# The first token group of a state-space block with a PReLU layer, put in another order

## The chip, the cores and the metric

The kernel runs on one core of a Trainium2 chip. The metric is the device time of one execution in microseconds. Five engines with a queue of their own each work in parallel: PE (matrix products), DVE (vector), ACT (scalar, activations), POOL (GpSimd) and SP (which issues most transfers). Each works through its own instructions strictly in order and waits for the others by semaphores.

## The reference

```
for each batch, head and chunk of 32 steps (4 batches, 8 heads, 768 steps):
    L     = exp(cum_i - cum_j), lower triangle, cum = running sum of log(clip(a, 1e-6, 1))
    y     = (C B^T * L) x  +  (C state) * exp(cum)
    state = exp(sum) * state + sum_j B_j x_j exp(cum_end - cum_j)
x2  = y as a (3072 tokens x 256) matrix, heads side by side
h   = x2 @ w_in                                  # 256 x 2048
g   = max(h, 0) + alpha * min(h, 0)              # PReLU, alpha per column
out = g @ w_out                                  # 2048 x 256
```

The weights w_in and w_out arrive as 64-bit floating-point numbers, the other arrays as 32-bit ones. The result is 32-bit.

## The kernel before

**Tiling.** The kernel works with its own chunks of 128 steps, 24 of them, two to a pair. Two pairs make a group of 512 tokens, and there are six groups. The state-space part of a pair gives its 256 columns of the matrix xT (features x tokens). When a group's xT is whole, the PReLU layer runs on it. Groups 1 to 5 use a product with fewer multiplications (`quad`, in four stretches for each group, with sums and differences of weights and tokens). Group 0 is different, because the weights are still arriving: it runs plain products, one tile of 128 hidden columns after another. All the changes concern group 0 and the loading that goes on beside it.

**Weights.** The weights come in 16 pieces of 512 KB. Pieces 0, 1 and then 2, 4, 6, 8, 10, 12 are parts of w_in (two tiles of hidden columns each), and 3, 5, 7, 9, 11, 13, 14, 15 are parts of w_out (two tiles each). Six buffers (`raw`) hold pieces as they land. A piece is turned into 32-bit numbers by several engines in turn: `convert_a` (ACT L238, then POOL L240, and ACT L245 or two L248), `sign` (DVE L259), `convert_b` (DVE L269) and the final addition in `convert` (POOL L291). The function `convert_next` finishes the next piece and, when its buffer is free again, issues the load of the piece six further on. Called with `first` it also begins `convert_a` two pieces ahead.

**First two pairs.** `first_two` computes pairs 0 and 1 by hand-written order, and with them the first two hidden tiles in halves (`hidden_two`: matmul L870, ACT L876, DVE L882). Its helpers are `turned` (transposes of B and C, copied by ACT into bc and cz), `gram_of` (L679), `added` (L688), `mask` (POOL L695), `copied` (ACT L703), `times` (L708 on POOL or DVE), `decays` (DVE scan L712) and `outputs` (L727, L735, and the copies to xT at L740; `warm` puts idle products ahead of them).

**The loop over tiles.** After that a loop runs over tiles f = 4 to 15. In each round come `hidden(0, f)` (matmul L855, ACT L858, DVE L859), some stages of the next pair (`ssm`: transposes L550, state L513 and L526, decay scans L470, gram L599, L609, outputs L628 and L636), the conversion of weight pieces, and `output` of the tile four earlier (L893). Two buffers (`hp`) take the hidden products, so tile f + 2 waits until DVE has read tile f, and a pair's gram borrows one of the two. Pair 2 and pair 3 are computed in this loop, for group 1.

**Later rows.** The decay factors of batches 2 and 3 come from a tile `rows` by clamping and two scans (`rows_clamp`, `rows_scan`, `rows_out`: L372 to L393). Their results go to memory, and pairs from 6 on read them from there. In the kernel before this happens in round 8 of the loop.

**Order.** There is no scheduler: every engine's instructions stand in the order in which the code issues them. SP issues nearly all loads in one queue. Names with one buffer number can be reused only when their readers are done.

Of the kernel before, what the change touches and what calls it, by code (L numbers as in the profile page):

```python
# [9 lines left out]
F32 = mybir.dt.float32  # L10
# [12 lines left out]
def kernel(  # L23
# [25 lines left out]
    nc = tc.nc  # L49
# [69 lines left out]

    def load_rows(i):  # L120

        rows = ld.tile([RW, Q], F32, name="rows")
        nc.sync.dma_start(out=rows, in_=a.rearrange("b h (c t) -> (b h c) t", t=Q)[i * RW : (i + 1) * RW])
        loads["r", i] = rows
# [15 lines left out]
    def load_pair(gp, decays=True):  # L140
# [8 lines left out]
        if gp == 0:  # L149
            load_a(ap, b, c, nc.scalar)  # L150
        elif gp >= NB:
            rows = scratch["pf", b // 2].rearrange("(b h c) t -> b h (c t)", b=2, h=H)
            rows = rows[b % 2, :, c * Q : (c + 2) * Q]
            nc.sync.dma_start(out=ap, in_=rows.unsqueeze(1).to_broadcast([H, N, 2 * Q]))
        if gp == 0:
            load_rows(0)
            nc.sync.dma_start(out=al_n, in_=moe_alpha.rearrange("(k p) -> k p", p=P))
# [326 lines left out]
    def pair(gp):  # L484
# [9 lines left out]
        def decays(k):  # L494

            for w in range(2):
                half_decays(k, w)
# [84 lines left out]
        else:  # L582
            states(added(ss_tile()))
            c_decayed()
            decays(0)
            yield
            decays(1)
            spread_c()

# [59 lines left out]
    def first_two():  # L649
# [43 lines left out]
        def mask(sm, new, ks):  # L693
            n = ks.stop - ks.start
            nc.gpsimd.tensor_tensor(  # L695
                out=sm[:, ks].rearrange("p k (g m) -> p k g m", g=2),
                in0=new[:, ks].unsqueeze(2).to_broadcast([P, n, 2, 2 * D]),
                in1=hmask.rearrange("p (g m) -> p g m", g=2).unsqueeze(1)
                .to_broadcast([P, n, 2, 2 * D]), op=ALU.mult)
# [64 lines left out]
        for r in range(4):  # L764
# [15 lines left out]
               for i in range(2)]  # L780
# [4 lines left out]
        nc.scalar.copy(out=new[0][:, 0], in_=dps[0][:, 0])  # L785
        sm0 = work.tile([P, 2, P], F32, name="sm")
        times(0, 0, g0, nc.gpsimd)
        mask(sm0, new[0], slice(0, 1))
        g1 = copied(gram[1])
        times(0, 1, g1, nc.gpsimd)  # L790
        convert_a(*pieces[0])
        times(0, 2, gram[2])
# [7 lines left out]
        convert_a(*pieces[1])  # L800
        outputs(0, (ss(), ss()), (None, sm0[:, 0]), cd0, xt0, (1, 0), 2)
        mask(sm0, new[0], slice(1, 2))
        bn1 = bn_of(1)

        sign(*pieces[0])
# [3 lines left out]
        convert_next()  # L809
        slope_signs()  # L810
        sign(*pieces[1])
        decays(1, 0, sp[1][0])
        convert_b(*pieces[1])
        tp = spare()
        bc1, cz1 = turned(nat1, tp)
        cd1 = work.tile([P, 2, Q], F32, name="cd")
        nc.gpsimd.tensor_tensor(out=cd1.rearrange("p k t -> p (k t)"),
                                in0=bc1[:, 2:].rearrange("p k t -> p (k t)"), in1=pf1,
                                op=ALU.mult)
        added(dps[1], bn1, xt1)  # L820
        new[1] = work.tile([P, 2, 2 * D], F32, name="state")
        for k in range(2):
# [3 lines left out]
                                           in1=dps[1][:, k], op0=ALU.mult, op1=ALU.add)  # L826
        decays(1, 1, sp[1][1])
        prelus = [hidden_two(0, 0, 0, tp)]
        gram = gram_of(bc1, cz1, [bank(2), bank(3), ss(), ss()])
        g0 = copied(gram[0])  # L830
        convert_next(first=False)
        sm1 = work.tile([P, 2, P], F32, name="sm")
        mask(sm1, new[1], slice(0, 2))
        times(1, 0, g0, nc.gpsimd)
        for r in range(1, 4):
            times(1, r, gram[r])
# [4 lines left out]
        prelus[1]()  # L841
        outputs(1, (bank(0), bank(1)), (sm0[:, 1], sm1[:, 0]), cd1, xt1, (0, 1), 1)
        state[0] = new[1][:, 1]
# [314 lines left out]
    first_two()  # L1158
    convert_a(*pieces[3])
    convert_next(first=False)  # L1160
    hidden_two(0, 0, 2 * Q, spare())()
    rest = hidden_two(0, 2, 2 * Q, spare())
# [3 lines left out]
    bns[2] = pair_loads(2)  # L1166
    convert_next(first=False)
    in_steps = {8: 0, 10: 1, 12: 2, 14: 3}
    for f in range(FIRST, NF):
        if f in (5, 10):  # L1170
            load_pair(3 + f // 10)
        if f == 5:
            load_rows(1)
        hidden(0, f)
        if f <= 10:
            ssm(2)
        if f >= 9:
            ssm(3)
        for i in {FIRST: (5,), FIRST + 1: (6, 7)}.get(f, ()):
            convert_a(*pieces[i])  # L1180
        convert_next(first=f > FIRST)
        if f == 14:
            bns[4] = pair_loads(4)
        if f == 8:
            bns[3] = pair_loads(3)
        if f == 8:
            rows_clamp(1)
            held["pr"] = rows_scan(1)
            rows_out(1)
        output(f - FIRST)  # L1190
        if f in in_steps:
            weight_sums(wi, in_sums, 0, in_steps[f])
    early[0] = None
    token_sums(1)
    ssm(2 * GC // 2, 4)
# [93 lines left out]
```

## Time and profile before

| What | us |
|---|---|
| median of 10 runs | 363.36 |
| lowest and highest of 10 runs | 362.53 to 364.48 |
| the profiled execution | 363.79 |
| its span, from the first to the last instruction | 362.1 |
| first hidden matmul (L870) | 18.10 |
| first matmul of the loop (L855, tile 4) | 29.12 |
| first matmul of group 1 (L979) | 82.69 |

The profile is of one execution. A row of a timeline gives the start, the duration (of all instructions merged in it), the engine, the line of the program, the operation, the output and the inputs, shapes, and in square brackets how long the engine was idle before it and what ended that. A row of waits gives the waiting engine, tile and line, what it waited for, the total, the number of waits and the longest. A row of the table by stretches gives the limits of the stretch and their length, the busy time of PE, of PE's weight loads, of DVE, ACT and POOL with the number of instructions of each, the granted clock of PE, the share in which the DMA engines were busy, and GB/s.

### The profile page before, as it was taken

Reading aid. Unit: us, or ns where it says so; the run is one execution under the profiler, and the core shown is the slowest. Engines: PE = TensorE matmul, PEld = TensorE weight load, DVE = VectorE, ACT = ScalarE, POOL = GpSimd, SP = SyncE. Lnnn points to the kernel's source line nnn. Section 1 sums busy time; section 2 is a strip of 40 time slices with the busy share of each in tenths; the row PEclk is TensorE's granted clock in tenths of the full one; section 3 lists DMA queues with packets and bytes.
Section 4 is the critical chain, followed back from the end, with each engine's and each line's share of the span. In section 5 each row is a group of like instructions: output and inputs, shape, how many; then the busy total and the mean of one; then the engine's idle time right before and its main releaser. Section 6 shows DMA issues by size and latency. Waiting matters only on the chain.

```text
span 362.1 us, 6726 instructions
## 1 busy us (share of the span) xinstructions
PE 352.5 (97%) x2511; PEld 287.6 (79%) x2511; DVE 248.3 (69%) x465; ACT 170.2 (47%) x367; POOL 202.4 (56%) x212
## 2 busy tenths in 40 slices
PE   8899889999999999999999999999999999999995
PEld 8576556668888888888888888888888888888884
DVE  6987699978837857867757867668867634643363
ACT  3667755625354345345345345345345344443431
POOL 4975547679847956626636526537536535444521
PEclk9999999999999999999999999999999999999999
DMA  7999899822066401003703602702701001001004
GB/s 131 192 187 314 273 246 236 181 81 58 31 134 140 105 2 59 2 2 58 171 5 56 159 21 48 181 6 49 159 29 29 2 2 29 0 3 29 0 0 89
DMA packets 111017, 31.67 MB, mean 87 GB/s; under 512 B 79289, under 2 KB 106889, under 8 KB 110985
## 3 DMA queue, kind: packets, MB, share of 16 engines
q1 hardware_dynamic: 110032, 30.92, 36.6%
q8 instruction: 20, 0.33, 0.4%
q10 hardware_dynamic: 952, 0.33, 0.4%
q14 instruction: 13, 0.10, 0.1%
HBM read 27.89 MB, written 3.34 MB: 86 GB/s over the span
## 4 chain that ended last, share of the span: by engine, by line
PE 88%; DMA 4%; DVE 2%; SPq 2%; ACT 2%; POOL 1%; issue 0%; POOLq 0%; DVEq 0%; ACTq 0%
PE bank L954 33%; PE hp L979 28%; PE bank L893 6%; PE ss L979 6%; DMA raw<-in_moe_w_in_dram 4%; PE hp L855 4%; PE ss L636 3%; PE ss L599 2%; PE hp L870 2%; PE ss L628 1%; SPq L163 1%; DVE dec L470 1%; PE ss L513 1%; ACT wt L238 1%; ACT wg L245 0%
## 5 line engine op out<-in xcount | busy, mean ns | idle before, releaser
L1036 POOL TENSOR_TENSOR gt<-gt 128x512 f32<-128x512 f32 x58 | 74.2, 1279 | 21.2 <-DVE gt L964 16.4
L954 PE MATMUL bank<-gt,w_out 128*128 128x256 f32 x320 | 83.5, 381 | 0.0
L954 PEld LDWEIGHTS bank<-gt,w_out 128*128 128x128 f32 x320 | 60.1, 190 | 10.2 <-issue 2.3
L1026 POOL TENSOR_TENSOR gt<-gt 128x512 f32<-128x512 f32 x20 | 25.4, 1272 | 67.5 <-DVE gt L964 62.1
L964 DVE SCALAR_TENSOR_TENSOR gt<-hp,s_mul,gt 128x256 f32<-128x256 f32 x96 | 42.0, 479 | 29.7 <-ACT gt L962 27.5
L954 PE MATMUL bank<-gt,ws 128*128 128x256 f32 x240 | 59.5, 379 | 0.0
L962 ACT ACTIVATE gt<-hp,s_alpha 128x256 f32<-128x256 f32 x96 | 40.4, 472 | 39.6 <-PE hp L979 25.9
L954 PEld LDWEIGHTS bank<-gt,ws 128*128 128x128 f32 x240 | 45.6, 190 | 6.2
L470 DVE TENSOR_TENSOR_SCAN dec<-abc,bank 128x256 f32<-128x256 f32 x80 | 48.4, 660 | 0.0
L979 PE MATMUL hp<-xs,w_in 128*128 128x256 f32 x160 | 41.9, 384 | 0.0
L979 PE MATMUL hp<-xs,ws 128*128 128x256 f32 x160 | 41.1, 379 | 0.0
L1005 DVE TENSOR_TENSOR hp<-hp,u 128x512 f32<-128x512 f32 x20 | 14.0, 698 | 29.0 <-ACT u L1003 29.0
L979 PEld LDWEIGHTS hp<-xs,ws 128*128 128x128 f32 x160 | 30.4, 190 | 4.1
L979 PEld LDWEIGHTS hp<-xs,w_in 128*128 128x128 f32 x160 | 29.7, 190 | 4.6 <-issue 0.2
L893 PE MATMUL bank<-w_out,gt 128*128 128x256 f32 x128 | 31.0, 384 | 0.0
L893 PEld LDWEIGHTS bank<-w_out,gt 128*128 128x128 f32 x128 | 23.7, 190 | 6.4 <-issue 3.3
L979 PE MATMUL ss<-xT,w_in 128*128 128x256 f32 x96 | 24.7, 380 | 0.2 <-DVE state L526 0.2
L855 PE MATMUL hp<-xT,w_in 128*128 128x512 f32 x48 | 22.8, 597 | 1.3 <-DVE gt L859 1.1
L529 POOL TENSOR_TENSOR sm<-state,bmask 128x256 f32<-128x256 f32 (+1 forms) x10 | 6.2, 619 | 29.5 <-DVE state L526 29.4
L994 ACT COPY m<-hp 128x512 f32<-128x512 f32 x8 | 4.7, 586 | 37.6 <-PE hp L979 37.6
L1003 ACT COPY u<-hp 128x512 f32<-128x512 f32 x20 | 11.7, 586 | 20.0 <-PE hp L979 20.0
L979 PE MATMUL hp<-xT,ws 128*128 128x256 f32 x80 | 20.5, 379 | 0.0
(178 smaller groups left out, 583.8 us busy)
## 6 DMA issues: line engine op xcount, KB each, us to landing
abc<-z SPq DMA_DIRECT2D x20, 512.0 KB
raw<-in_moe_w_in_dram SPq DMA_DIRECT2D x8, 512.0 KB
raw<-in_moe_w_out_dram SPq DMA_DIRECT2D x8, 512.0 KB
xt<-in_x_dram SPq DMA_DIRECT2D x24, 128.0 KB
nat<-in_B_dram SPq DMA_DIRECT2D x38, 64.0 KB
out_dram<-o_sb SPq DMA_DIRECT2D x32, 64.0 KB
nat<-in_C_dram SPq DMA_DIRECT2D x24, 64.0 KB
ap<-pf SPq DMA_DIRECT2D x11, 128.0 KB
```

What stands on the lines that cost most here:

```text
L470: nc.vector.tensor_tensor_scan(out=dv[:, k, hs], data0=abc[k][:, hs], data1=ident_p[0], initial=0.0, op0=ALU.mult, op1=ALU.add)
L636: nc.tensor.matmul(y[w][32 * q : 32 * q + 32, k], xt[:, k, h * D : (h + 1) * D], dec[:, k, h], start=False, stop=True, tile_position=(0, 3 ...
L855: nc.tensor.matmul(hp, w_in[:, k, f * P : (f + 1) * P], xts[g][:, k], start=(k == 0), stop=(k == KC - 1))
L893: nc.tensor.matmul(pos[0][t // 2][:, t % 2], gt[:, t * Q : (t + 1) * Q], w_out[:, f], start=(f == 0 and t % 2 == 0), stop=(f == NF - 1), s ...
L954: nc.tensor.matmul(ms[g][i][:, h], w, blocks[g, z][n][:, p], start=(q == 0 and h == 0), stop=(q == NQ - 1), skip_group_check=True)
L962: nc.scalar.mul(o[:, p], h[:, p], s_alpha[:, fs[p]])
L964: nc.vector.scalar_tensor_tensor(out=o[:, p], in0=h[:, p], scalar=s_mul[:, fs[p]], in1=o[:, p], op0=ALU.mult, op1=ALU.max)
L979: nc.tensor.matmul(to[:, p], w(2 * z + p), b, start=start and p == 0, stop=True, skip_group_check=True)
L1003: nc.scalar.copy(out=u2, in_=A)
L1005: nc.vector.tensor_tensor(out=Y, in0=Y, in1=u2, op=ALU.add)
L1026: nc.gpsimd.tensor_tensor(out=tc_, in0=g22, in1=g12, op=ALU.subtract)
L1036: eng.tensor_tensor(out=o, in0=x0, in1=x1, op=ALU.subtract)
```

## The change

Several things are altered. The order of POOL's, DVE's and PE's work in `first_two` is different: piece 0 is converted between two other POOL operations, `bn1`, the second mask and the slope signs come later, the first hidden product comes ahead of `added`, and the warm product of the second outputs is gone. Right after `first_two`, the sign of piece 3 is taken ahead of two PReLU parts. The masked state of pair 0 lies in two tiles of one chunk each. In the loop, a table `CONVERTED` says in which round, and whether ahead of the pair's stages (0) or behind them (1), a piece begins (a string) or is finished (a number); in the old order pieces 6, 7 and 8 were begun in round 5. Decay scans of the later rows move from round 8 to round 14. In `pair`, `spread_c` stands ahead of the scans. Pair 4's state product goes to half of bank 3, and the first two loads (`ap`, `rows`) swap their queues, SP and ACT.

```diff
--- before.py
+++ after.py
@@ -117,10 +117,10 @@
     loads = {}
-    def load_rows(i):
+    def load_rows(i, eng=nc.sync):
         rows = ld.tile([RW, Q], F32, name="rows")
-        nc.sync.dma_start(out=rows, in_=a.rearrange("b h (c t) -> (b h c) t", t=Q)[i * RW : (i + 1) * RW])
+        eng.dma_start(out=rows, in_=a.rearrange("b h (c t) -> (b h c) t", t=Q)[i * RW : (i + 1) * RW])
         loads["r", i] = rows
     scratch = {}
@@ -147,13 +147,13 @@
         ap = ldx.tile([P, 2 * Q], F32, name="ap")
         if gp == 0:
-            load_a(ap, b, c, nc.scalar)
+            load_a(ap, b, c)
         elif gp >= NB:
             rows = scratch["pf", b // 2].rearrange("(b h c) t -> b h (c t)", b=2, h=H)
             rows = rows[b % 2, :, c * Q : (c + 2) * Q]
             nc.sync.dma_start(out=ap, in_=rows.unsqueeze(1).to_broadcast([H, N, 2 * Q]))
         if gp == 0:
-            load_rows(0)
+            load_rows(0, nc.scalar)
             nc.sync.dma_start(out=al_n, in_=moe_alpha.rearrange("(k p) -> k p", p=P))
         abc = []
         later = []
@@ -582,10 +582,10 @@
         else:
             states(added(ss_tile()))
             c_decayed()
+            spread_c()
             decays(0)
             yield
             decays(1)
-            spread_c()
@@ -693,7 +693,7 @@
         def mask(sm, new, ks):
             n = ks.stop - ks.start
             nc.gpsimd.tensor_tensor(
-                out=sm[:, ks].rearrange("p k (g m) -> p k g m", g=2),
+                out=sm.rearrange("p k (g m) -> p k g m", g=2),
                 in0=new[:, ks].unsqueeze(2).to_broadcast([P, n, 2, 2 * D]),
                 in1=hmask.rearrange("p (g m) -> p g m", g=2).unsqueeze(1)
                 .to_broadcast([P, n, 2, 2 * D]), op=ALU.mult)
@@ -783,12 +783,12 @@
         g0 = copied(gram[0])
         new[0] = work.tile([P, 2, 2 * D], F32, name="state")
         nc.scalar.copy(out=new[0][:, 0], in_=dps[0][:, 0])
-        sm0 = work.tile([P, 2, P], F32, name="sm")
+        sm0 = [prep.tile([P, 1, P], F32, name=f"sm{k}") for k in range(2)]
         times(0, 0, g0, nc.gpsimd)
-        mask(sm0, new[0], slice(0, 1))
+        mask(sm0[0], new[0], slice(0, 1))
         g1 = copied(gram[1])
+        convert_a(*pieces[0])
         times(0, 1, g1, nc.gpsimd)
-        convert_a(*pieces[0])
         times(0, 2, gram[2])
         times(0, 3, gram[3])
         nc.vector.scalar_tensor_tensor(out=new[0][:, 1], in0=new[0][:, 0],
@@ -798,40 +798,38 @@
         sp.append(spread(z1, 1, bank))
         xts[0] = xtp.tile([P, KC, GT], F32, name="xT")
         convert_a(*pieces[1])
-        outputs(0, (ss(), ss()), (None, sm0[:, 0]), cd0, xt0, (1, 0), 2)
-        mask(sm0, new[0], slice(1, 2))
-        bn1 = bn_of(1)
-
+        outputs(0, (ss(), ss()), (None, sm0[0][:, 0]), cd0, xt0, (1, 0), 2)
         sign(*pieces[0])
         decays(0, 0, sp[0][0])
         convert_b(*pieces[0])
         decays(0, 1, sp[0][1])
         convert_next()
-        slope_signs()
-        sign(*pieces[1])
-        decays(1, 0, sp[1][0])
-        convert_b(*pieces[1])
         tp = spare()
         bc1, cz1 = turned(nat1, tp)
+        bn1 = bn_of(1)
+        decays(1, 0, sp[1][0])
+        sign(*pieces[1])
+        convert_next(first=False)
         cd1 = work.tile([P, 2, Q], F32, name="cd")
         nc.gpsimd.tensor_tensor(out=cd1.rearrange("p k t -> p (k t)"),
                                 in0=bc1[:, 2:].rearrange("p k t -> p (k t)"), in1=pf1,
                                 op=ALU.mult)
+        mask(sm0[1], new[0], slice(1, 2))
+        prelus = [hidden_two(0, 0, 0, tp)]
         added(dps[1], bn1, xt1)
+        decays(1, 1, sp[1][1])
         new[1] = work.tile([P, 2, 2 * D], F32, name="state")
         for k in range(2):
             e = (k + 1) * Q - 1
             old = new[1][:, 0] if k else new[0][:, 1]
             nc.vector.scalar_tensor_tensor(out=new[1][:, k], in0=old, scalar=pf1[:, e : e + 1],
                                            in1=dps[1][:, k], op0=ALU.mult, op1=ALU.add)
-        decays(1, 1, sp[1][1])
-        prelus = [hidden_two(0, 0, 0, tp)]
         gram = gram_of(bc1, cz1, [bank(2), bank(3), ss(), ss()])
         g0 = copied(gram[0])
-        convert_next(first=False)
         sm1 = work.tile([P, 2, P], F32, name="sm")
         mask(sm1, new[1], slice(0, 2))
         times(1, 0, g0, nc.gpsimd)
+        slope_signs()
         for r in range(1, 4):
             times(1, r, gram[r])
         convert_a(*pieces[2])
@@ -839,7 +837,7 @@
         prelus[0]()
         convert_next(first=False)
         prelus[1]()
-        outputs(1, (bank(0), bank(1)), (sm0[:, 1], sm1[:, 0]), cd1, xt1, (0, 1), 1)
+        outputs(1, (bank(0), bank(1)), (sm0[1][:, 0], sm1[:, 0]), cd1, xt1, (0, 1))
         state[0] = new[1][:, 1]
         masked[0] = sm1[:, 1]
         early[0] = 16
@@ -1157,14 +1155,19 @@
     FIRST = 4
     first_two()
     convert_a(*pieces[3])
+    sign(*pieces[3])
+    hidden_two(0, 0, 2 * Q, spare())()
     convert_next(first=False)
-    hidden_two(0, 0, 2 * Q, spare())()
     rest = hidden_two(0, 2, 2 * Q, spare())
     convert_a(*pieces[4])
     rest()
     identity_bank()
     bns[2] = pair_loads(2)
     convert_next(first=False)
+
+    CONVERTED = {(4, 1): ("5", 5), (5, 1): ("6", 6), (6, 1): ("7",), (7, 0): ("8", 7), (7, 1): (8,),
+                 (8, 1): ("9", 9, "10"), (9, 1): (10, "11", 11), (10, 1): ("12",),
+                 (11, 1): (12, "13"), (12, 1): (13, "14"), (13, 1): (14, "15"), (14, 1): (15,)}
     in_steps = {8: 0, 10: 1, 12: 2, 14: 3}
     for f in range(FIRST, NF):
         if f in (5, 10):
@@ -1172,25 +1175,29 @@
         if f == 5:
             load_rows(1)
         hidden(0, f)
-        if f <= 10:
-            ssm(2)
-        if f >= 9:
-            ssm(3)
-        for i in {FIRST: (5,), FIRST + 1: (6, 7)}.get(f, ()):
-            convert_a(*pieces[i])
-        convert_next(first=f > FIRST)
+        for part in range(2):
+            if part:
+                if f <= 10:
+                    ssm(2)
+                if f >= 9:
+                    ssm(3)
+            for i in CONVERTED.get((f, part), ()):
+                if isinstance(i, str):
+                    convert_a(*pieces[int(i)])
+                else:
+                    convert_next(first=False)
         if f == 14:
             bns[4] = pair_loads(4)
-        if f == 8:
-            bns[3] = pair_loads(3)
-        if f == 8:
             rows_clamp(1)
             held["pr"] = rows_scan(1)
             rows_out(1)
+        if f == 8:
+            bns[3] = pair_loads(3)
         output(f - FIRST)
         if f in in_steps:
             weight_sums(wi, in_sums, 0, in_steps[f])
     early[0] = None
+    beside[GC] = m5_bank[0][:, : 2 * Q]
     token_sums(1)
     ssm(2 * GC // 2, 4)
```

## The prediction

> **What bounds the kernel now.** I read the page first, then PE's own waits up to 85 us, then the chain of waits and the timelines of ACT, DVE and POOL over the stretches where PE waits. The page gives the bound, the windows table where it holds:
>
> ```profile
> PE 352.5 (97%) x2511; PEld 287.6 (79%) x2511; DVE 248.3 (69%) x465; ACT 170.2 (47%) x367; POOL 202.4 (56%) x212
> 0.00:18.00 18.00, 15.42 (x202) 12.57 (x202) 14.49 (x27) 8.89 (x18) 12.90 (x26) 1.00 0.83 161
> 29.00:48.00 19.00, 16.30 (x77) 10.23 (x77) 14.38 (x24) 14.00 (x26) 10.14 (x13) 1.00 0.93 265
> 48.00:82.00 34.00, 34.00 (x262) 21.71 (x263) 29.19 (x47) 17.03 (x31) 22.76 (x25) 1.00 0.75 189
> 100.00:362.00 262.00, 258.28 (x1767) 219.91 (x1765) 165.89 (x325) 115.23 (x261) 132.06 (x125) 1.00 0.25 54
> ```
>
> From 48 us on PE has no gap to speak of. (The 3.7 us missing from the last row are the end of the program.) So the end of the program is the moment at which PE runs freely, plus a fixed amount of PE work. Only time that PE loses before 48 us can be won. PE's waits there:
>
> ```profile
> PE ss L599 <- ACT cz L560: 1.5, 1, 1.5
> PE hp L855 <- DVE gt L859: 1.1, 1, 1.1
> PE hp L688 <- POOL bn L418: 0.6, 1, 0.6
> PE hp L870 <- POOL w_in L291: 0.6, 1, 0.6
> PE hp L855 <- DVE gt L882: 0.2, 1, 0.2
> PE ss L979 <- DVE state L526: 0.2, 1, 0.2
> ```
>
> The two longest have one cause, which ACT's timeline shows:
>
> ```profile
> 36.79 0.68 ACT L238 ACTIVATE wt<-raw 128x512 f32<-128x512 f32 x1 [1.11 <-DMA raw<-in_moe_w_in_dram]
> 38.16 0.69 ACT L238 ACTIVATE wt<-raw 128x512 f32<-128x512 f32 x1
> 41.08 0.68 ACT L238 ACTIVATE wt<-raw 128x512 f32<-128x512 f32 x1 [1.20 <-DMA raw<-in_moe_w_in_dram]
> 42.24 0.66 ACT L858 ACTIVATE gt<-hp,s_alpha 128x512 f32<-128x512 f32 x1
> 42.81 0.89 ACT L560 ACTIVATE cz<-bc,par 128x256 f32<-128x256 f32 x2
> ```
>
> The rows at 36.79, 38.16 and 41.08 convert weight pieces 6, 7 and 8. Tile 6's PReLU (L858 at 42.24) stands behind them in ACT's queue. PE had finished tile 6 at about 38.7, so ACT sat on finished work until piece 8 had landed at 41.0. Behind it waited cz (PE's 1.46 us before L599) and DVE's half of the PReLU at 42.94. Behind that, on DVE, four scans of 2.4 us and piece 7 delayed tile 7's PReLU to 47.05, which is the 1.12 us before tile 8's matmul at 47.94.
>
> **Part 1: the start, up to the first hidden matmul (18.10).** That matmul waits for POOL's L291 of piece 0 (16.60, 1.45 us). POOL's queue runs L708 (10.51), mask (11.74), L708 (12.16), two L240 (13.69), mask (15.59), bn (16.00), L291. In the changed order the first L240 comes ahead of the second L708, and mask and bn (0.46 + 0.64) follow L291. From the same durations: mask ends 12.20, L240 (0.65) 12.85, L708 (1.45) 14.3, second L240 (0.65 to 1.1) 15.2, L291 (1.45) 16.6. DVE's L269 finds its input at 12.85 instead of 14.34 and is done by 14.3. The second L708 ends 0.7 us later, but the outputs that read it are the eleventh to sixteenth of 16 products that start at 14.44, so they don't see it. What is late next: the matmul writes the bank of the turned tiles, which ACT copies out from 16.14 to 16.73. So it starts at about 16.8: gain 1.3.
>
> The eight L688 now follow it on PE instead of lying in an idle stretch: 0.43 us lost (row of 9.75, 16 halves). Their xt landed by 17.2 and bn is ready at 17.25. The keep-warm matmul of the second outputs goes: 0.43 us gained. In the old order gram, L870 and warm-up ran to 23.5; in the new one gram runs 19.2 to 20.3, the second L870 to 22.2 (its POOL piece 1 is done by about 19.2), L727 and L735 to 23.5 against 24.75. POOL's cd (0.72), two masks (0.46, 0.73) and L708 (1.28) end at 22.3, about 0.4 ahead of need. ACT's copies then release the next four L870 pairs at about 23.6, or 24.0 with some slip, against 25.20: gain 1.2 to 1.6.
>
> **Part 2: PReLU ahead of conversions (tiles 4 to 8).** Matmul durations stay: 1.72 a tile, 1.73 an output. Tile 4 at 27.4 without its 0.2 wait. Piece 4 landed at about 29.2 by the trace's landing events, so ACT gives tile 4's PReLU only at 30.7 to 31.3, but tile 6 needs that at 35. Then output 0, tile 5, L513, output 1, tile 6 (35.0 to 36.7), output 2, tile 7 (38.4 to 40.1). ACT is now: cz (spread_c stands a stage earlier) by 35.1, piece 6 at 36.8 (a landing that I leave where it is) to 38.0, tile 6's PReLU 38.0 to 38.6, piece 7 to 40.3, tile 7's PReLU to 40.9. L599 finds cz done for 5 us and its bank free at about 39.6: the 1.46 goes. DVE: L269 of piece 6 by 39.0, PReLU 6, four scans (2.4) to 42.0, PReLU 7 to 42.7. Tile 8 can start at 43.0, where PE arrives: the 1.12 goes.
>
> What is late next is a floor set by the landing of piece 6: it carries DVE to 42.7, piece 7's L259 and L269 to 43.8, and POOL's L291 to 45.1. Output 4 needs that and PE is there at 44.75. So output 4 starts at 45.1 against 49.89 before: 4.8 us ahead. The floor also means that a larger or smaller gain in part 1 hardly shows.
>
> **Part 3: conversions ended a tile sooner, scans moved.** Rows' L372, L379, L381, L391, L393 (53.65 to 56.19, 2.5 us of DVE) go from tile 8 to tile 14, past six tiles. At tile 14 DVE finished at 78.6 and waited 1.88 us for ACT; it is about 2 us further ahead of PE in the new order, so the 2.5 us fit ahead of PReLU 15 within 0.3 us, and no matmul before the group's end reads that tile. If that cover is gone they cost up to 2.5 us there. Their two DMAs (48 KB each) leave SP's queue ahead of pair 4's eight loads, which no longer wait from 53.4 to 56.2, and now stand ahead of pair 5's ten, which start at about 74 instead of 63.5. Pair 5's bn was used at 93.72 and will be at about 89. Its loads took 8.8 us to issue on queues 94% busy, and the share falls to 0.18 after 80 us, so they are in by about 84: nothing. The same slack hides the reordering of pieces 9 to 15. Piece 3's sign (one L259) moves ahead of a pair of L882 on DVE, into a stretch where DVE idles 0.51 us before 27.25 for POOL: nothing.
>
> **Part 4: small ones.** Pair 4's state goes to bank 3, so the first L979 no longer waits for DVE's L526: 0.23. The slope signs (0.63 + 0.25) move behind POOL's L708; ACT's L248 needs them at 24.6, they end at 23.2: nothing. The swap of ap and rows between SP and ACT isn't shown by the trace. An ap-sized issue on SP took 0.76 (L130 at 5.79), rows 0.41, so everything behind it on SP is 0.35 later. Upper end 0.35, lower end 0, since DVE takes rows at 3.36, behind other work, and ap only after it. I take 0.1, because nat landed at 6.4 just as PE came to it, and the floor of part 2 absorbs it.
>
> **A rule against this change.** L259 takes 0.40 us by its shortest row and 1.01 at 25.74, where POOL's L291 ran from 25.19 to 26.47; over the group it averages 0.70. The Trainium skill, "SBUF — State Buffer", section "Who interferes with whom", says that a two-port VectorE operation and a GpSimd operation block each other for the whole instruction. By the rule each conversion that is packed tightly behind the other engine's costs up to 1.27 more. Pieces 7 and 8 stand ahead of the first outputs of pair 2 at 48.6, for which DVE is done at about 48.0 with 0.4 per free L259. By the row (0.3 more each) this just fits; by the rule, both blocked, 2.5 more, which is 1.9 us of new wait. I take the row: only one of the two meets an L291 by my times.
>
> **The sum.** 45.1 against 49.89 is 4.8, 0.23 more at the first L979, less some 0.2 for waits between engines that a hand-made schedule leaves out: 4.8. The profiled execution took 363.79 us (span 362.1), which gives 359.0. The ten runs' median is 363.36, 0.43 below it, which gives 358.6.
>
> **The rivals.** First, part of the gain is taken back in the dense stretch from tile 8 to tile 15, by the port as above (1.9) or by landings later than now: gain 2 to 3, 361.0. For it: DVE was 98% busy from 60 to 70 us. Against: PE never waited there, and DVE has 2.5 us of scans less to do. Second, the start loses instead (rows from ACT late, POOL's first L240 slowed): at most 0.4 to 1, since the floor of part 2 stays; 359.4. Third, slower: SP's queue. Pair 5's loads wait behind rows' z until DVE reaches tile 14. POOL takes pair 5's bn in order at about 89 us, with three L1036 behind it that PE's products read. Every microsecond of landing after 89 is a microsecond of PE; beyond 94 it eats the whole gain, and at 96 gives 365. It decides if z is issued after 84 instead of 74. Against: DVE would have to be 10 us behind. That the change doesn't do what it says is excluded for the main part: the new order has tile 6's PReLU ahead of piece 7's conversion on ACT.
>
> **How the numbers follow.** The forecast has 0.66, the first rival 0.18, the second 0.10, the third and other losses 0.06. Range: 357.5 (part 1 in full, no slip) to 361.0 (first rival). A measurement here tells 0.2% (0.7 us) from no change. Gains of 2 us and more are faster: 0.92; 0.02 lies within; 0.06 slower.
>
> **What would show it.** PE's waits before L599 and before L855 in front of tile 8 are gone; ACT's L858 of tile 6 starts at about 38; the first L870 starts at 16.8; output 4 starts at about 45; PE is gapless from there; the first L979 starts at about 77.8. It is wrong if a wait on DVE or POOL appears between 45 and 78, if L979 stays above 80, or if POOL idles before pair 5's bn.

## The result, and the profile after

The kernel after the change takes 360.09 us, median of 15 runs (359.87 to 362.58), against 363.12 us for the kernel before on the same chip (50 runs, 361.99 to 365.37). The ratio is 0.9921, 95% interval 0.9907 to 0.9934: 2.9 us faster. 358.6 was forecast, with 357.5 to 361.0 as the range, so the direction and the range held and the gain was forecast too large: 4.8 against 3.0.

The profiled execution after took 360.08 us. First the page of the kernel after, its line of busy times:

```profile
PE 352.1 (98%) x2509; PEld 287.5 (80%) x2509; DVE 247.5 (69%) x465; ACT 169.4 (47%) x367; POOL 202.9 (57%) x212
```

PE's work is what it was (352.5 before, with two products more). It stands closer together, as the table by stretches of the kernel after shows (columns as before):

```profile
29.00:48.00 19.00, 19.00 (x88) 12.18 (x87) 16.81 (x29) 12.69 (x24) 12.33 (x14) 1.00 0.97 274
48.00:82.00 34.00, 34.00 (x268) 22.35 (x267) 28.86 (x49) 18.46 (x35) 25.64 (x28) 1.00 0.61 158
```

In the stretch from 29 to 48 us PE had been busy for 16.30 of 19 us; now it is busy for all 19.00. The waits of PE up to 85 us in the kernel after:

```profile
PE hp L299 <- PEq L1280: 0.8, 1, 0.8
PE hp L868 <- ACT bc L667: 0.8, 1, 0.8
PE ss L679 <- ACT cz L670: 0.3, 1, 0.3
PE bank L453 <- POOL z L428: 0.2, 1, 0.2
PE hp L853 <- DVE gt L880: 0.2, 1, 0.2
```

The lines have moved: L853, L856 and L857 are the old L855, L858 and L859 (a tile's matmul and its PReLU), L868 is the old L870, L874 and L880 are L876 and L882, L891 is L893, L977 is L979. The 1.5 us before L599, the 1.1 us before tile 8's matmul and the 0.2 us before L979 are gone. Why, ACT's timeline of the kernel after shows:

```profile
34.83 0.93 ACT L560 ACTIVATE cz<-bc,par 128x256 f32<-128x256 f32 x2
36.97 0.67 ACT L238 ACTIVATE wt<-raw 128x512 f32<-128x512 f32 x1 [1.22 <-DMA raw<-in_moe_w_in_dram]
...
38.12 0.66 ACT L856 ACTIVATE gt<-hp,s_alpha 128x512 f32<-128x512 f32 x1
38.70 0.66 ACT L238 ACTIVATE wt<-raw 128x512 f32<-128x512 f32 x1
```

ACT still stands idle until piece 6 has landed (36.97). But behind that piece tile 6's PReLU now comes next, at 38.12 instead of 42.24, and piece 7's conversion (38.70) comes behind it. cz is ready at 35.8, long before L599 at 41.33.

The same marks in two profiles of each kernel (the second ones are the runs e10_before_again and e9_after_again, below):

| mark | before | before again | after | after again |
|---|---|---|---|---|
| first hidden matmul (L870, now L868) | 18.10 | 18.57 | 17.18 | 16.90 |
| tile 4's matmul | 29.12 | 29.59 | 28.23 | 27.85 |
| tile 8's matmul | 47.94 | 46.45 | 44.24 | 43.86 |
| first matmul of group 1 (L979, now L977) | 82.69 | 81.81 | 78.68 | 78.12 |
| profiled execution's time | 363.79 | 362.91 | 360.08 | 359.67 |

Between the first profile of each, group 1 begins 4.0 us sooner, the span is 4.2 us shorter (362.1 to 357.9) and the time 3.7 us. From L979 to the last instruction the two kernels run alike (279.2 to 279.4 us in all four profiles). What differs is the time that lies outside the span: by the median of the runs 1.7 us in before and 2.2 in after. It is 2.2 in e1, e4, e6 and e8 too, 1.6 and 1.7 in e3 and e7, 1.8 in e2 and e5, and 2.0 and 1.9 in e11 and e12. So 0.4 to 0.5 us of what the new order wins is lost again outside the span; what causes that is not shown.

### The profile page after: what moved, and what is told of

Its sections match the earlier page's. It is cut to its first block, busy times and chain, and to the rows that moved or that the text cites. A ratio compares the mean times of both kernels' runs of the same rounds, so it can differ in the third digit from the quotient of the medians.

```text
span 357.9 us, 6719 instructions
## 1 busy us (share of the span) xinstructions
PE 352.1 (98%) x2509; PEld 287.5 (80%) x2509; DVE 247.5 (69%) x465; ACT 169.4 (47%) x367; POOL 202.9 (57%) x212
## 4 chain that ended last, share of the span: by engine, by line
PE 93%; DVE 3%; POOL 1%; issue 1%; ACT 0%; POOLq 0%; DVEq 0%
PE bank L952 34%; PE hp L977 28%; PE bank L891 8%; PE hp L853 6%; PE ss L977 6%; PE ss L636 3%; PE ss L599 2%; PE ss L628 1%; PE hp L299 1%; DVE dec L765 1%; DVE dec L712 1%; DVE wr L269 1%; PE hp L868 1%; PE bank L441 1%; PE ss L513 1%
## 5 line engine op out<-in xcount | busy, mean ns | idle before, releaser
L952 PEld LDWEIGHTS bank<-gt,ws 128*128 128x128 f32 x240 | 45.6, 190 | 6.2
L977 PE MATMUL hp<-xs,w_in 128*128 128x256 f32 x160 | 41.9, 384 | 0.0
L977 PE MATMUL hp<-xs,ws 128*128 128x256 f32 x160 | 41.2, 380 | 0.0
L977 PEld LDWEIGHTS hp<-xs,ws 128*128 128x128 f32 x160 | 30.3, 190 | 4.3 <-POOL xs L932 0.2
L977 PEld LDWEIGHTS hp<-xs,w_in 128*128 128x128 f32 x160 | 29.7, 190 | 4.6 <-issue 0.2
L891 PE MATMUL bank<-w_out,gt 128*128 128x256 f32 x128 | 31.1, 385 | 0.0
L891 PEld LDWEIGHTS bank<-w_out,gt 128*128 128x128 f32 x128 | 23.6, 190 | 6.7 <-issue 3.1
L977 PE MATMUL ss<-xT,w_in 128*128 128x256 f32 x96 | 24.6, 379 | 0.0
L853 PE MATMUL hp<-xT,w_in 128*128 128x512 f32 x48 | 22.7, 596 | 0.2 <-DVE gt L880 0.2
L977 PE MATMUL hp<-xT,ws 128*128 128x256 f32 x80 | 20.5, 379 | 0.0
```

The source lines that it names most:

```text
L853: nc.tensor.matmul(hp, w_in[:, k, f * P : (f + 1) * P], xts[g][:, k], start=(k == 0), stop=(k == KC - 1))
L891: nc.tensor.matmul(pos[0][t // 2][:, t % 2], gt[:, t * Q : (t + 1) * Q], w_out[:, f], start=(f == 0 and t % 2 == 0), stop=(f == NF - 1), s ...
L952: nc.tensor.matmul(ms[g][i][:, h], w, blocks[g, z][n][:, p], start=(q == 0 and h == 0), stop=(q == NQ - 1), skip_group_check=True)
L977: nc.tensor.matmul(to[:, p], w(2 * z + p), b, start=start and p == 0, stop=True, skip_group_check=True)
```

## The experiments

Each kernel was compared with the kernel before on its own chip, where the median of before was 363.12 (after), 363.39 (e1 to e4), 364.04 (e5, e6, e8, e11) and 363.21 (e7, e9, e12). The table has all of them. Two columns carry most of the reading: when tile 4's matmul starts (what the start gave), and how long it is from there to the first L979 (what the loop gave), both from the profile of the run. The clock column counts runs whose mean granted PE clock was below 0.997; more on it in the last section.

| kernel | median us | ratio to before [95%] | clock below 0.997 | tile 4 | tile 4 to L979 |
|---|---|---|---|---|---|
| before | 363.12 | 1 | 32 of 80 | 29.12, 29.59 | 53.57, 52.22 |
| after | 360.09 | 0.9921 [0.9907, 0.9934] | 1 of 15 | 28.23 | 50.45 |
| e1_loads_back | 360.27 | 0.9916 [0.9897, 0.9936] | 0 of 6 | 28.62 | 50.30 |
| e2_loop_only | 364.63 | 1.0038 [1.0023, 1.0053] | 13 of 17 | 30.05 | 52.99 |
| e3_first_only | 363.22 | 0.9984 [0.9965, 1.0003] | 2 of 14 | 28.52 | 52.44 |
| e4_rows_back | 363.17 | 0.9996 [0.998, 1.0011] | 2 of 14 | 28.38 | 53.38 |
| e5_loop_rows | 363.12 | 0.9977 [0.9954, 1.0] | 9 of 14 | 29.48 | 50.78 |
| e6_rows_early | 361.36 | 0.9936 [0.9913, 0.9958] | 0 of 6 | 28.41 | 51.09 |
| e7_rows_only | 362.68 | 0.9988 [0.9974, 1.0002] | 7 of 14 | 31.44 | 51.37 |
| e8_warm | 361.41 | 0.9942 [0.9921, 0.9964] | 2 of 10 | 30.36 | 50.29 |
| e9_after_again | 359.81 | 0.9911 [0.9892, 0.993] | 0 of 6 | 27.85 | 50.27 |
| e11_start | 360.52 | 0.9913 [0.989, 0.9935] | 0 of 6 | 28.74 | 50.29 |
| e12_start | 359.69 | 0.991 [0.9889, 0.9931] | 0 of 6 | 27.94 | 50.26 |

**One part at a time.** e3_first_only gives the kernel before the new `first_two` and piece 3's early sign, and nothing else:

```diff
         times(0, 0, g0, nc.gpsimd)
...
         g1 = copied(gram[1])
-        times(0, 1, g1, nc.gpsimd)
         convert_a(*pieces[0])
+        times(0, 1, g1, nc.gpsimd)
...
+        prelus = [hidden_two(0, 0, 0, tp)]
         added(dps[1], bn1, xt1)
```

> The kernel before with the first two pairs' part of the change alone: the new order there, the mask in two tiles and piece 3's sign. The loop, its scans, the loads and the bank stay as before. The first L870 starts at about 16.8 and tile 4 at 28. Theory 1: in the old loop tile 6's PReLU waits for piece 8's landing at 41, so the start's 1.2 us end in a longer wait before L599: 0 to 0.3 us off, 363.0. Rival, the parts add up: 1.2 us off, 361.9.

It came out at 363.22, ratio 0.9984 with 1 inside the interval: no gain that can be told. Its runs spread from 361.65 to 364.24, and the profiled one, with 361.77, is among the shortest. In its trace tile 4 starts 0.6 and 1.1 us sooner than in the two profiles of before. PE's waits of e3_first_only show what the new start leaves in place:

```profile
PE hp L853 <- DVE gt L857: 1.3, 2, 1.1
```

The 1.1 us is the wait before tile 8 (at 45.91), where a PReLU is late in the old loop's order. The other 0.2 us stands before a later tile (67.61), on a chain that goes back to a wait of DVE for a load, which the next run makes plain. Where the slower runs of e3 lose the rest is not shown.

e2_loop_only gives the kernel before the table `CONVERTED` and the early `spread_c` alone; the rows stay in round 8:

```diff
+            spread_c()
             decays(0)
...
-            spread_c()
...
-        for i in {FIRST: (5,), FIRST + 1: (6, 7)}.get(f, ()):
-            convert_a(*pieces[i])
-        convert_next(first=f > FIRST)
+        for part in range(2):
...
+            for i in CONVERTED.get((f, part), ()):
```

> The kernel before with the loop's part of the change alone: the table of conversions in the loop and the earlier spread of C. The first two pairs, the later rows' scans, the loads and the bank stay as before. Theory 1, PE's own path: the waits before L599 and tile 8 go, tile 4 stays at 29.1, so tile 8 starts at about 45.2 instead of 47.9: 2.7 us off, 360.4. Theory 2, landing floor: output 4 at 45.1 to 46, and nearly the whole gain is here: 360.1. Rival: the gain needs both parts, since the first part's late PReLUs hold the loop: under 1.5 us.

It was slower than before: 1.0038, interval above 1. In part that is a lowered clock, which 13 of its 17 runs show (last section). PE's waits of e2_loop_only, and below them a row of its DVE timeline:

```profile
PE hp L688 <- DMA xt<-in_x_dram: 1.5, 2, 0.9
PE hp L855 <- DVE gt L859: 1.1, 1, 1.1
PE hp L599 <- DVE gt L859: 0.5, 1, 0.5
```

```profile
54.82 0.22 DVE L372 TENSOR_SCALAR r<-rows 96x128 f32<-96x128 f32 x1 [2.91 <-DMA rows<-in_a_dram]
```

The 1.5 us for xt belongs to the start. The main mechanism works here too: the waits before L599 of pair 2 (at 43.75 in before) and before tile 8 are gone. The two waits for L859 in this list stand later, at 65.58 (L599 of pair 3) and 69.68. They come from DVE, which now stands 2.91 us at L372, the first instruction on the later rows, because their load has not landed. In the first profile of before DVE reached L372 at 53.65 without any idle time. In the second (e10_before_again) it stood there too, as its DVE timeline shows:

```profile
53.99 0.40 DVE L372 TENSOR_SCALAR r<-rows 96x128 f32<-96x128 f32 x1 [1.74 <-DMA rows<-in_a_dram]
```

So the rows' load was close already in the old order. This is a wait that the prediction did not have.

e7_rows_only moves the rows' scans to round 14 in the kernel before, and nothing else (the edit is that of e5 below).

> The kernel before with only the later rows' scans moved to round 14. In the old order DVE reached the rows at 53.65, about when they had landed, and did not wait, so by the theory of the rows' landing the move alone buys little: within 0.7 us of the kernel before. Rival, the 2.5 us of DVE in round 8 cost by themselves, whatever the rest: 1 to 2 us off.

0.9988, with 1 just inside the interval: 0.4 us by the ratio, and no gain that can be told. But 7 of its 14 runs had a lowered clock, against 3 of 19 of before on this chip; the runs with a full clock have medians of 362.3 and 363.3. So the move alone may be worth up to 0.9 us. That would fit the second profile of before, where DVE stood 1.74 us for the rows and PE lost 0.5 us at 68.45, at the end of the profile's chain from that wait.

**The rows' scans put back.** e4_rows_back is the kernel after with the rows in round 8 again:

```diff
         if f == 14:
             bns[4] = pair_loads(4)
+        if f == 8:
+            bns[3] = pair_loads(3)
+        if f == 8:
             rows_clamp(1)
             held["pr"] = rows_scan(1)
             rows_out(1)
-        if f == 8:
-            bns[3] = pair_loads(3)
```

> The changed kernel with the later rows' scans put back to round 8 of the loop, and nothing else. Theory 1: DVE has the 2.5 us free in round 8 too, because it waits 3.1 us for POOL at 54 anyway, and PE needs tile 9's PReLU only at 57.7: no change, within 0.3 us of 360.1. Rival: DVE is the next bound in the dense stretch, and 1 to 2 us come back as a wait of PE between tiles 9 and 13: 361.5.

The whole gain goes: 363.17, ratio 0.9996. DVE's timeline of e4_rows_back, at the place where tile 9's PReLU (L857) is due:

```profile
49.83 0.69 DVE L269 SCALAR_TENSOR_TENSOR wr<-wt,wr 128x512 uint32<-128x512 uint32 x1
53.92 0.22 DVE L372 TENSOR_SCALAR r<-rows 96x128 f32<-96x128 f32 x1 [3.40 <-DMA rows<-in_a_dram]
...
54.97 0.75 DVE L857 SCALAR_TENSOR_TENSOR gt<-hp,s_mul,gt 128x512 f32<-128x512 f32 x1
```

and the same place in DVE's timeline of the kernel after:

```profile
49.56 0.69 DVE L269 SCALAR_TENSOR_TENSOR wr<-wt,wr 128x512 uint32<-128x512 uint32 x1
50.50 0.75 DVE L857 SCALAR_TENSOR_TENSOR gt<-hp,s_mul,gt 128x512 f32<-128x512 f32 x1 [0.24 <-ACT gt L856]
```

The order of instructions on DVE is fixed, so everything behind L372 waits with it: tile 9's PReLU is 4.5 us later, then the parts of the next pieces (the next L269 with an idle stretch ahead of it ends at 60.8 instead of 57.7), then the PReLUs behind those. PE's waits of e4_rows_back:

```profile
PE hp L853 <- DVE gt L857: 1.3, 2, 1.1
PE hp L599 <- DVE gt L857: 0.5, 1, 0.5
```

That is 1.8 us of waiting, out of the 2.9 us that the loop takes longer. A further 0.7 us or so is lost at L599 without a wait of its own. In the kernel after its 16 products overlap and take 1.1 us (62.76 to 63.83). In e4 six of them start from 63.50 on, and the one that needs an `hp` buffer and the nine behind it only at 64.68, so that the next output comes 2.2 us after the first. The remaining 0.4 us lies in longer steps around the three waits.

e6_rows_early separates the landing from the scans. It is e4 with the rows' load issued in `first_two`, 20 us earlier:

```diff
         load_spread(2, *divmod(4, CPB))
+        load_rows(1)
...
-        if f == 5:
-            load_rows(1)
```

> e4 (the changed kernel with the later rows' scans in round 8) with their load issued early, in the first two pairs ahead of the weight pieces 4 and up, so that it has landed long before. The scans stay in round 8. Theory, the rows' landing: DVE no longer waits at L372 and its 1.1 us of scans find room: 360.3. Rival, DVE's work in round 8 is what costs: 362.5 to 363, as in e4.

361.36, ratio 0.9936: of the 3.0 us that e4 lost, 1.8 come back (2.2 by the ratios). DVE's timeline and PE's waits of e6_rows_early (here L858 is the PReLU):

```profile
50.20 0.22 DVE L372 TENSOR_SCALAR r<-rows 96x128 f32<-96x128 f32 x1
```

```profile
PE hp L854 <- DVE gt L858: 0.7, 1, 0.7
```

DVE reaches L372 with no idle time, and one wait of 0.7 us is left, with the scans' own work still ahead of tile 9's PReLU. So the larger part of what the move to round 14 saves is the wait for a load, the smaller part the work of the scans in round 8.

**Loop and rows without the new start.** e5_loop_rows is e2 with the rows in round 14:

```diff
-        if f == 8:
-            bns[3] = pair_loads(3)
-        if f == 8:
             rows_clamp(1)
             held["pr"] = rows_scan(1)
             rows_out(1)
+        if f == 8:
+            bns[3] = pair_loads(3)
```

> The loop's part as in e2 together with the move of the later rows' scans to round 14, on the kernel before; the first two pairs, the loads and the bank as before. Theory, the rows' landing: in e2 and e4 DVE stood 2.9 and 3.4 us at L372 for the rows' load and PE paid 1.5 us of it before L599 and at the tile after; without that the loop's part shows what it is worth: 2.5 to 3 us off the kernel before, 360.6. Rival, the first pairs' order is needed as well: within 1 us of the kernel before.

By median it is 363.12, ratio 0.9977 with 1 at the end of the interval. But its runs fall into two heaps: five of 361.17 to 361.65, nine of 363.02 to 365.89. The profiled one took 361.36. PE's waits in it:

```profile
PE hp L688 <- DVE wr L259: 0.5, 1, 0.5
PE hp L688 <- DMA xt<-in_x_dram: 0.5, 1, 0.5
PE ss L979 <- DVE state L526: 0.3, 1, 0.3
```

Nothing is left of the waits in the loop: tile 4 to L979 takes 50.78, where the kernel after takes 50.45. So in the five shorter runs the loop part together with the rows is worth about 1.9 us (361.36 against 363.2), and the new start the remaining 1.3. Why the nine others are 2 us longer is taken up in the last section.

**Does the landing of piece 6 set a floor?** The prediction said that output 4 could not start before 45.1, since the landing of piece 6 carries DVE and POOL to that time, so that a smaller gain at the start would hardly show. e8_warm tries it: the kernel after, with four warm products (0.96 us of PE in its trace) ahead of the second outputs.

```diff
-        outputs(1, (bank(0), bank(1)), (sm0[1][:, 0], sm1[:, 0]), cd1, xt1, (0, 1))
+        outputs(1, (bank(0), bank(1)), (sm0[1][:, 0], sm1[:, 0]), cd1, xt1, (0, 1), 2)
```

> The changed kernel with two keep-warm matmuls of 0.43 us put ahead of the second pair's outputs, which delays PE there by 0.8 us and changes no result. Theory 1, PE's own path: the delay comes through to the end: 360.9, tile 8 at 45.0. Theory 2, the prediction's floor at output 4 (piece 6's landing): up to 0.8 us are absorbed, 360.1 to 360.3.

The ratio is 0.9942 against 0.9921 and 0.9911 of the kernel after: 0.8 to 1.1 us more, the size of the products, though the intervals overlap. The trace adds where it shows. PE's timeline of e8_warm has

```profile
30.36 1.10 PE L853 MATMUL hp<-xT,w_in 128*128 128x512 f32 x2 [0.21 <-DVE gt L880]
```

for tile 4, 2.13 us later than the kernel after. Of that, 1.36 us had been lost ahead of the added products (its first hidden matmul came at 18.54). From tile 4 to L977 it took 50.29 against 50.45. So the delay is passed on whole, and nothing at 45.1 takes it up. What would hold PE if it came to output 4 sooner than 45.6 us, the earliest in these profiles, was not tried.

**Small parts, and an attempt at more.** e1_loads_back is the kernel after with the first two loads on their old queues:

```diff
-            load_a(ap, b, c)
+            load_a(ap, b, c, nc.scalar)
...
-            load_rows(0, nc.scalar)
+            load_rows(0)
```

> The changed kernel with only the first two loads put back (ap on ACT, rows on SP). In the changed profile everything from the first transposes on is 0.3 us later than before (first gram at 8.99 against 8.67, last load of pair 1's C landing at 15.9 against 15.5). Theory 1, PE's own path: after 17.2 us PE never waits, so the 0.3 us at the start come through to the end: 359.8 against 360.1, first L868 at 16.85 to 16.9. Theory 2, the landing floor of the prediction: output 4 is held by piece 6's landing, so the start does not show: 360.1, whatever the first L868 does.

360.27, ratio 0.9916: the same as the kernel after. The swap does nothing that can be measured, and the first L679 starts between 8.47 and 9.35 us in the profiles here, with this code either way.

e11_start takes up what is late next, PE's 0.8 us ahead of the first L868. The first hidden product writes another buffer than the turned tiles do, POOL finishes piece 0 ahead of clamping piece 1, and the mask and cd come ahead of piece 1's addition. e12_start differs from it in one place: cd goes behind that addition.

```diff
-        convert_a(*pieces[1])
+        convert_a(*pieces[1], clamp=False)
...
         convert_next()
+        clamped(parts[id(pieces[1][0])][1])
         tp = spare()
+        tz = ss()
...
-        prelus = [hidden_two(0, 0, 0, tp)]
+        prelus = [hidden_two(0, 0, 0, tz)]
...
-        gram = gram_of(bc1, cz1, [bank(2), bank(3), ss(), ss()])
+        gram = gram_of(bc1, cz1, [bank(2), bank(3), ss(), tp])
```

> An attempt to better the changed kernel at its one remaining wait of 0.77 us (first L868): that product goes to another bank than the turned tiles, POOL adds piece 0 ahead of clamping piece 1, and the second mask and cd come ahead of piece 1's addition, in POOL's idle 1.2 us. Theory 1, PE's own path: first L868 at 16.6 and 0.5 us off the changed kernel, 359.6. Rival: the outputs of pair 1 are set by DVE's second sign and POOL's last product, which do not move: 0 to 0.2 us, 360.0.

> e11 with cd put back behind piece 1's addition, since in e11 cd waited for a load and held up that addition, which cost PE 0.95 us at the second L868. Theory 1, PE's own path: 0.4 to 0.6 us under the changed kernel on the same chip. Rival: the start is set by loads that land at another moment in each run, and the two stay within 0.2 us.

The first hidden matmul of e11 did start sooner, at 16.87, but PE then waited 0.9 us at the second one for POOL's piece 1, because cd held POOL. Tile 4 came at 28.74. e12 removes most of that; PE's waits of e12_start (its L874 is the hidden product):

```profile
PE ss L874 <- POOL w_in L295: 0.5, 1, 0.5
PE hp L874 <- DVE state L831: 0.5, 1, 0.5
```

Two waits of 0.5 stand in place of one of 0.8, tile 4 is at 27.94 (27.85 in the unaltered kernel on the same chip), and 359.69 against 359.81 is no difference. No version was found that beats the kernel after.

The last two repeat the kernel after and the kernel before, unaltered.

> The changed kernel again, unaltered, as the measure for the next one on the same chip: 360.1.

> The kernel before again, one look. If its times from 362 to 365 come from loads landing at other moments, this profile has other waits of PE up to 85 us than the first: the waits before L688 for xt, before L599 and before the tile after it change by 0.5 us or more, and nothing after 85 us does.

The repeat of after (0.9911) agrees with the first. The repeat of before (one run, 362.91 us) shows other waits than its first profile did:

```profile
PE hp L855 <- DVE gt L859: 1.2, 2, 0.7
PE hp L870 <- POOL w_in L291: 1.0, 1, 1.0
```

The wait of 1.5 us before L599, on which the prediction built most of Part 2, is not among them, and one of the two waits of L855 (0.5 us, at 68.45) stands behind the rows' load. So PE's waits in the old order differ from execution to execution, and one profile shows one draw. That the landing of the pieces decides which waits come is argued, not shown.

## Why the prediction was right, and where it was not

**What holds PE (right in the main).** In the kernel after PE has no gap behind tile 4's 0.2 us, and L979 came 4.0 us sooner, the last matmuls 3.9 (358.12 to 354.25). That only time lost before 48 us could be won holds for the first profile of before; in the second PE lost 0.5 us at 68.45.

**Part 2, PReLU ahead of conversions (mechanism right).** Tile 6's PReLU was forecast at 38.0 and came at 38.12; both long waits went. Its floor was wrong. Piece 7's addition was due at 45.1 whatever the start did, and PE was to wait for it. In e9, after and e8 that L291 ended at 45.43, 45.97 and 47.94, and output 4 came at 45.58, 46.03 and 48.08. PE's row shows no wait, but it was close: output 4's weight load waited 0.6 to 0.7 us for the addition, and in the kernel after the step from tile 8 to output 4 took 1.79 us, where it took 1.72 and 1.71 in the other two. Piece 6's landing did not set it: in the kernel after DVE's rows show no idle time from 34.87 to 50, so piece 7's parts came when the work queued ahead of them on DVE was done.

**Part 1, the start (size).** The first hidden matmul came at 17.18 and 16.90, where 16.8 was forecast. In the first of the two profiles it waited for the reason named, ACT's copy of the turned tiles, in the second for POOL's L291 of piece 0. No floor takes up what is lost at the start, so the rest of PE's path counts, and it was summed too short. From there to tile 4 the kernel after took 11.05 us, against 10.6 forecast. The 0.2 us wait before tile 4 stayed. ACT's copies of the second outputs began 6.7 us behind the first hidden matmul, as forecast, but the next hidden products came 0.43 us behind that (23.87 to 24.30, and 24.77 to 25.20 in before), where the forecast had 0.1 (23.5 to 23.6). Nor was POOL 0.4 us ahead of need: its L708 ended at 23.10, and L735 began right behind it at 23.16. From tile 4 to tile 8 the kernel after took 16.0 against 15.6: from start to start, a tile or an output takes the 1.71 to 1.73 of the sum only next to another of its kind, and 1.79 to 1.83 beside the products of a pair, of which five steps here are examples. So the start of output 4 was 46.03, 0.9 later than forecast, and L977 at 78.68 was 0.9 later too.

**Part 3, the rows costed at nothing (the step that failed).** It asked only whether 2.5 us of DVE would fit in at the new place. They did: the kernel after has no wait there, and pair 5's later loads cost nothing either. It did not ask what the scans would do at the old place once tiles came 3 us sooner. e2 and e4 show it: DVE would stand 2.9 to 3.4 us for the rows' load (and in the second profile of before it stood 1.7 already). The step carries 3.0 of the 3.0 us, in the sense that without it nothing is left. The sum took the price of the move at its new place for the whole effect of the move.

**The parts do not add.** Singly they gave −0.2 per cent at the most (start), −0.1 (rows) and +0.4 (loop); in the pair e5 −0.2, in the pair e4 nothing; all three −0.8. In e2 the gain of the loop went into DVE's wait for the rows, which the third part removes; in e3 the wait before tile 8 stayed, which the loop removes. The lowered clock has a share in these figures, above all in e2 and e5 (last section).

**Part 4 (right within what can be told).** The 0.2 us before L979 is there in the profiles of before, e2, e3, e5 and e7, none of which has the new bank, and in none with it. The swap of loads, put at 0.1 lost, is nothing.

**From profile to median.** Profile against profile the gain was 3.7, where 4.8 was summed. PE's path to L979 was 0.9 longer than forecast; the end of the span made up 0.2 to 0.3 of that, and some 0.5 was lost outside the span, which the sum had taken as fixed. The remaining 0.7 is the profiled run of before, 363.79, which lay 0.67 above the median of the 50 runs beside the kernel after. The prediction knew only ten runs and allowed 0.43.

**The rivals.** The measured 360.09 lies nearer to the figures of the first two rivals than to 358.6, but not for their reasons. The first (361.0) expected a give-back between tiles 8 and 15 by the port or by late landings. PE has no wait there, so it did not occur. The second (359.4) put the loss at the start; some 0.8 us are indeed missing by tile 4, but for other reasons than it gave, and with no floor that limits them. The third needed POOL to stand before pair 5's bn; SP issued the rows' z and pf at 77.9 and 78.3 and pair 5's B, C and x by 84.3, and bn ran at 90.05 with no idle time on POOL ahead of it.

**The port rule against the row.** The row was taken, and single instructions are nearer to the rule. In the kernel after, L269 takes 0.69 us in free places, and here, first in its DVE timeline and then in POOL's,

```profile
13.85 1.32 DVE L269 SCALAR_TENSOR_TENSOR wr<-wt,wr 128x512 uint32<-128x512 uint32 x1
```

```profile
13.34 1.27 POOL L708 TENSOR_TENSOR dec<-o_sb,dec 128x512 f32<-128x512 f32 x1
```

it took 1.32, from inside POOL's product to its end at 14.61 and 0.56 beyond: 0.6 us more, twice what the row gave. In the dense stretch the lengthened ones fell where DVE had slack, such as the 3.08 us in which it waited for POOL ahead of the L269 at 57.04. The rule's 1.9 us of new wait did not come.

## What to carry to other kernels

When an in-order queue is freed sooner, list what it now reaches sooner, and for each the landing of what that reads: here a load that was just in time in one profile of the kernel before, and 1.7 us late in another, became a stop of 3.4 us for everything behind it. Weigh a moved step twice, for what it costs at the new place and for what it would cost if it stayed. Measure parts of such a change in pairs as well as singly, for none of the three parts here showed a clear gain by itself, and take a second profile of the kernel before you build a sum on one wait.

## What the runs showed of the hardware

**The granted clock can halve after gaps of under 1 us.** The table by stretches of e7_rows_only (granted clock is the third figure from the end):

```profile
16.00:17.00 1.00, 0.48 (x3) 0.14 (x1) 1.00 (x2) 0.34 (x2) 1.00 (x2) 1.00 1.09 171
17.00:18.00 1.00, 0.32 (x8) 0.19 (x8) 1.00 (x2) 0.97 (x3) 0.92 (x2) 1.00 0.94 205
18.00:19.00 1.00, 0.46 (x9) 0.37 (x10) 1.00 (x2) 0.25 (x1) 0.39 (x2) 1.00 0.96 330
19.00:20.00 1.00, 1.00 (x4) 0.80 (x4) 0.96 (x4) 0.00 (x0) 0.74 (x1) 0.58 0.82 240
20.00:21.00 1.00, 1.00 (x4) 0.82 (x3) 1.00 (x2) 0.00 (x0) 1.00 (x2) 0.50 0.94 344
21.00:22.00 1.00, 1.00 (x3) 0.44 (x2) 0.41 (x1) 0.00 (x0) 1.00 (x2) 0.50 1.13 248
22.00:23.00 1.00, 1.00 (x13) 0.78 (x16) 0.00 (x0) 0.65 (x2) 0.25 (x1) 0.72 0.81 113
```

From 16 to 19 us PE is busy for 1.26 of 3 us, and then it runs at half clock for some 3.4 us. Its timeline shows the price: eight products of the first hidden tile take 3.46 us,

```profile
18.54 0.32 PE L688 MATMUL hp<-xt,bn 128*32 128x64 f32 x8 [0.85 <-DMA xt<-in_x_dram]
18.79 3.46 PE L870 MATMUL hp<-xT,w_in 128*128 128x256 f32 x8
```

where they take 1.99 elsewhere (e5_loop_rows). The longest single gap is 0.85 us. The Trainium skill, "TensorE: Matmul & The Clock Gate", section "What's actually happening", has the clock halve after an idle window of about 3.4 us; here the clock halved without one. In the other profiles with the old start PE was busy for a little more of these 3 us (1.42 in the second of before, 1.46 in e2, 1.64 in the first of before, 1.86 in e5), and the clock stayed at 1.00; in the kernel after it was 2.23. The page also says that the window runs freely, so that an order could be hit in one execution and spared in the next. Whether the share of busy time or the place of the window decides is not told apart by these runs.

**What that makes of the times.** The kernels with the old start (before, e2, e5, e7) had a mean granted clock below 0.997 in 61 of 125 runs, those with the new start in 7 of 83. In e5 the two heaps are parted by it: the five runs below 362 us have 0.997 to 0.999, the nine above 363 have 0.990 to 0.996, and their medians lie 2.0 apart, near the 1.7 us that the half clock costs in e7 (0.42 + 0.50 + 0.50 + 0.28 by the rows above). In the old order L688 stands ahead of the first hidden product and waits for xt's landing; in the new one it stands behind it. So the new start has a further effect: it rarely loses the clock. (e3, which has the new start alone, lost it in 2 of 14 runs.) That the place of L688 is the reason is argued, not shown. For before the runs with a full clock have a median of 363.2, the others 363.9, so there a part of the loss is taken up later. That the dip lies at this place in those runs too is argued from e7's profile, not shown, since no other run with a mean below 0.997 was profiled. Why e2 was hit in 13 of 17 runs stays open.

**A scan beside POOL.** In e4, where POOL was idle, the scan L381 took

```profile
54.19 0.42 DVE L381 TENSOR_TENSOR_SCAN pr<-r,ends 96x128 f32<-96x128 f32 x1
```

and in the kernel after, beside POOL's L291 (75.46, 1.27 us), it took

```profile
75.48 1.52 DVE L381 TENSOR_TENSOR_SCAN pr<-r,ends 96x128 f32<-96x128 f32 x1
```

It took 1.47 in the first profile of before as well. With the second scan (0.40 in e4, 0.77 in before), some 1.4 of the 2.5 us that the prediction gave to the rows went with POOL's work beside them: in e4 the same instructions take 1.1 us in all.
